# A four-layer attention block on one core: layer sums regrouped, value staging moved, far masks shared with GpSimd, loads throttled

## The chip, the cores and the metric

The kernel runs on one core of one Trainium2 chip. The metric is the device time of one execution in microseconds (us), lower is better. Each figure is the median of several executions, and each kernel was run beside the kernel before on the same chip. Ratios are the mean time of one kernel's fast runs over the mean of the other's fast runs of the same rounds, so not quite the ratio of the medians quoted beside them. The span of a profiled execution is 1 to 3 us shorter than its time.

TensorE (PE in the profile) has two rows: matmuls (PE) and the loading of the stationary operand (PEld). VectorE is DVE, ScalarE is ACT, GpSimd is POOL, and SP issues transfers.

## The reference

Sequence 2048, width 512, 32 heads of 16. Layers 1 and 3 are linear attention (A), layers 2 and 4 are causal softmax attention over a window of 256 keys (B).

```python
def A(x, wqkv, wo):                      # q, k, v: 32 heads of 16
    phi = lambda t: where(t > 0, t + 1, exp(t)) + 1e-6
    pq, pk = phi(q), phi(k)
    kv = einsum("hsd,hse->hde", pk, v)   # a sum over all 2048 tokens
    z  = pk.sum(over tokens)
    o  = einsum("hqd,hde->hqe", pq, kv) / (einsum("hqd,hd->hq", pq, z) + 1e-6)
    return o @ wo
def B(x, wqkv, wo):
    s = q @ k.T / 4;  keep 0 <= query - key < 256
    return softmax(s) @ v @ wo
x = A_x
x = x + A(layernorm(x));  x = x + B(layernorm(x))
x = x + A(layernorm(x));  x = x + B(layernorm(x))
```

Because `kv` sums over all tokens, nothing of layer 3's output can start before layer 2 is complete: there is a barrier in the middle.

## The kernel before

The kernel is a list of operations, each with what it reads and writes. A compressed table (`TABLE`) fixes for all of them their order on each engine, the engine where there is a choice, and the PSUM bank. Tokens go in 16 tiles of 128. Per tile and layer B there are edge scores (two blocks of 64 keys, up to 256 queries each) and, for 14 tiles, far scores (64 queries per key block, at the far end of the window, with a triangular mask).

Layer A multiplies the query features by a reciprocal that one matmul group (`spread`) copies from 8 heads to 128 rows, tile by tile:

```python
def a_out(self, t, key):
    for f in range(4):        # 4 full-array matmuls of 128 columns
        e.matmul(K.ps(ps)[:, f*P:(f+1)*P], K.spread[:, tg, f, :], K.rec[:, G, :], ...)
    ... tensor_tensor(K.pqd, K.ps(ps), K.XQ[tile], ALU.mult)   # VectorE
```

The loads are issued one after another without waiting; the order is x0, x1, x2-3, wAk, x4-5, wAv, x6-7, wAq, the rest of x, then the other weights. In layer 1 each token tile has a key, a value and a query projection, and the keys times values are summed after that.

The softmax here doesn't subtract the row's maximum and nothing guards it: scores larger than these inputs give would overflow.

## Time and profile before

| | before |
|---|---|
| median of 4 runs of the comparison | 432.88 us (432.72 to 434.98) |
| span of the profiled run, mean granted clock | 432.7 us, 0.987 |
| ScalarE idle in the two attention stretches | 5.9 and 2.5 us |

I cut traces at four events: the first exponential of layer 2, the last one of it, the first of layer 4, the last of it. So the five windows are: start with the first layer, attention of layer 2, barrier, attention of layer 4, tail. The columns are the stretch and its length, then busy time and count of PE, PEld, DVE, ACT and POOL, then granted clock, DMA share and GB/s. Kernel before:

```profile
0.00:73.50 73.50, 63.43 (x683) 41.24 (x684) 62.46 (x140) 32.76 (x60) 39.91 (x83) 1.00 0.44 117
73.50:239.40 165.90, 160.76 (x3219) 102.48 (x3218) 154.16 (x353) 160.00 (x231) 22.22 (x52) 1.00 0.42 85
239.40:276.80 37.40, 37.13 (x600) 29.40 (x599) 30.21 (x67) 16.57 (x32) 9.56 (x18) 1.00 0.06 20
276.80:425.20 148.40, 137.21 (x3024) 90.35 (x3023) 124.48 (x273) 145.93 (x204) 11.64 (x25) 0.97 0.41 95
425.20:432.70 7.50, 3.54 (x62) 1.97 (x59) 3.41 (x8) 0.01 (x1) 0.00 (x0) 0.92 0.12 38
```

ScalarE is full in the second and fourth window (160.00 of 165.90, 145.93 of 148.40), TensorE in the third (37.13 of 37.40). A saving counts only in the window whose full engine it relieves.

### The profile page before, as it was taken

How to read it: one execution, taken by the hardware profiler on the slowest of the kernel's cores; microseconds unless marked ns; L12 is line 12 of the kernel's file. 1: busy time of each engine (PE TensorE's matmuls, PEld its weight loads, DVE VectorE, ACT ScalarE, POOL GpSimd, SP SyncE). 2: the span in 40 equal slices, each digit the busy share in tenths (PEclk: the TensorE clock that was granted, in tenths of full speed). 3: DMA queues.
4: the chain of work that ended last, by engine and by line, in shares of the span. 5: the costliest groups of instructions: out<-in, count | busy, mean ns of one | idle time of the engine just before them, and what ended most of it. 6: DMA issues, size and time to landing. Idle time of an engine off the chain costs nothing.

```text
span 432.7 us, 17332 instructions
## 1 busy us (share of the span) xinstructions
PE 402.1 (93%) x7576; PEld 265.4 (61%) x7576; DVE 374.7 (87%) x838; ACT 355.3 (82%) x525; POOL 83.3 (19%) x177
## 2 busy tenths in 40 slices
PE   1999999999999999999999999999999999999675
PEld 0555777655665665655656778765667576666443
DVE  5997799999999999988988679999899898987545
ACT  1454546999999999999998443799999999999982
POOL 7789112011120111111000141111000101000000
PEclk9999999999999999999999999999999999999869
DMA  7635104424443555545421000234344443436321
GB/s 241 220 64 148 49 2 106 97 65 97 117 84 82 78 102 101 89 78 107 97 53 26 15 3 2 88 102 102 91 105 94 105 102 101 90 100 101 92 53 51
DMA packets 69292, 37.84 MB, mean 87 GB/s; under 512 B 49248, under 2 KB 64608, under 8 KB 69216
## 3 DMA queue, kind: packets, MB, share of 16 engines
q1 hardware_dynamic: 69216, 36.73, 36.9%
q8 instruction: 60, 0.98, 1.0%
q14 instruction: 16, 0.13, 0.1%
HBM read 6.29 MB, written 2.10 MB: 19 GB/s over the span
## 4 chain that ended last, share of the span: by engine, by line
PE 43%; ACT 41%; DVE 9%; DMA 3%; issue 1%; POOL 1%; SPq 1%; POOLq 0%
ACT pb L549 31%; PE ps L351 19%; PE ps L365 10%; ACT pb L583 7%; PE ps L608 6%; PE ps L535 3%; DMA xres<-in_A_x_dram 2%; ACT pb L550 2%; PE ps L402 1%; DVE stats L312 1%; ACT tE L374 1%; DVE xres L478 1%; DMA xT<-xn 1%; DVE xn L316 1%; PE ps L573 1%
## 5 line engine op out<-in xcount | busy, mean ns | idle before, releaser
L549 ACT ACTIVATE pb<-ps 128x1024 bf16<-128x1024 f32 x224 | 211.1, 1050 | 3.7 <-PE ps L535 2.7
L608 PEld LDWEIGHTS ps<-vB,pb 128*128 128x128 bf16 x2880 | 80.3, 96 | 16.8 <-issue 3.9
L608 PE MATMUL ps<-vB,pb 128*128 128x34 bf16 x2880 | 86.8, 178 | 2.0 <-ACT pb L549 1.0
L314 POOL TENSOR_SCALAR ve<-mv 128x1 f32<-128x1 f32 x64 | 18.1, 283 | 285.3 <-DVE mv L313 284.1
L351 PE MATMUL ps<-wA,XQ 128*128 128x512 bf16 x256 | 65.9, 387 | 3.2 <-DMA wA<-in_A_wqkv_dram 2.8
L365 PE MATMUL ps<-xT,wBp 128*128 128x128 bf16 x1024 | 66.9, 219 | 1.6 <-DVE o L620 0.5
L374 ACT ACTIVATE tE<-ps 128x512 bf16<-128x512 f32 x64 | 38.1, 605 | 35.6 <-PE ps L351 16.9
L365 PEld LDWEIGHTS ps<-xT,wBp 128*128 128x128 bf16 x1024 | 58.2, 98 | 9.5 <-issue 1.7
L583 ACT ACTIVATE pb<-ps 128x512 bf16<-128x512 f32 x112 | 60.8, 642 | 1.6 <-PE ps L573 1.2
L556 DVE TENSOR_TENSOR pb<-pb,tri 128x512 bf16<-128x512 bf16 x128 | 52.2, 415 | 8.6 <-ACT pb L550 4.3
L535 PE MATMUL ps<-XQ,kB 32*128 32x256 bf16 (+3 forms) x1024 | 49.9, 270 | 8.4 <-ACT pb L550 2.6
L478 DVE TENSOR_TENSOR xres<-ps,xres 128x512 bf16<-128x512 f32 x64 | 43.7, 684 | 5.9 <-PE ps L351 5.4
L312 DVE BATCH_NORM_STATS2 stats<-xres 128x6 f32<-128x512 bf16 x64 | 43.6, 686 | 5.5 <-DMA xres<-in_A_x_dram 4.8
L590 DVE TENSOR_TENSOR pb<-pb,tri 128x1024 bf16<-128x1024 bf16 x56 | 37.5, 678 | 1.3 <-ACT pb L583 1.3
L315 POOL TENSOR_TENSOR rs<-ve,negh 128x1 f32<-128x1 f32 x64 | 37.6, 587 | 5.3
L535 PEld LDWEIGHTS ps<-XQ,kB 32*128 32x128 bf16 x1024 | 15.3, 92 | 37.7 <-ACT pb L549 17.9
L351 PEld LDWEIGHTS ps<-wA,XQ 128*128 128x128 bf16 x256 | 21.7, 98 | 26.4 <-issue 4.9
L351 PE MATMUL ps<-wBo,oT 128*128 128x512 bf16 x128 | 35.2, 388 | 1.3 <-DVE oT L335 0.5
L365 PE MATMUL ps<-XQ,wA 128*128 128x128 bf16 x512 | 35.5, 219 | 0.0
L351 PE MATMUL ps<-M,pqd 128*128 128x512 bf16 x128 | 34.6, 380 | 0.5 <-DVE pqd L472 0.5
L365 PEld LDWEIGHTS ps<-XQ,wA 128*128 128x128 bf16 x512 | 30.9, 98 | 6.6 <-issue 0.4
L351 PE MATMUL ps<-wBv,xT 128*128 128x512 bf16 x128 | 33.9, 381 | 0.7 <-DVE vA L495 0.4
(77 smaller groups left out, 453.7 us busy)
## 6 DMA issues: line engine op xcount, KB each, us to landing
vB<-vA SPq DMA_DIRECT2D x128, 68.0 KB, 2.1
kB<-vA SPq DMA_DIRECT2D x64, 128.0 KB, 2.1
out_dram<-xres SPq DMA_DIRECT2D x16, 128.0 KB, 2.5
wA<-in_A_wqkv_dram SPq DMA_DIRECT2D x3, 512.0 KB, 9.4
xres<-in_A_x_dram SPq DMA_DIRECT2D x2, 512.0 KB, 8.1
pb<-in_B_wqkv_dram SPq DMA_DIRECT2D x1, 1024.0 KB, 9.6
xres<-in_A_x_dram SPq DMA_DIRECT2D x3, 256.0 KB, 3.8
wBv<-in_B_wqkv_dram SPq DMA_DIRECT2D x1, 512.0 KB, 4.3
```

What stands on the lines that cost most here:

```text
L312: self.on("DVE", "stats", lambda e: e.bn_stats(K.stats[:, t, :], K.xres[:, t, :]), key, dve(512), rd=[("xres", t)], wr=[("stats", t)])
L315: self.on("POOL", "pow", lambda e: e.tensor_tensor(K.rs[:, t, :], K.ve[:, t, :], K.negh[:], ALU.pow), key + 0.03, (640, 690), rd=[("ve", t ...
L351: m = e.matmul(K.ps(ps), lhs(c), rhs(c), start=c == 0, stop=c == 3)
L365: m = e.matmul(K.ps(ps)[:, f * P:(f + 1) * P], w(c, f), xT(c), start=c == 0, stop=c == 3)
L374: self.on("ACT", "E", lambda e: e.activation(K.tE[:, s, :], K.ps(ps), ACT.Exp, bias=0.0), key, act(512), wr=[("tE", s)], ps=[ps])
L478: self.on("DVE", "res", lambda e: e.tensor_tensor(K.xres[:, t, :], K.ps(po), K.xres[:, t, :], ALU.add), key, dve(512), rd=[("xres", t)], w ...
L535: m = e.matmul(K.ps(ps[gq])[:, 256 * b:256 * b + ns[b]], K.kB[rows, j % 4, 2 * f + b, :, :], K.XQ[rows, f, q:q + ns[b]], start=True, stop= ...
L549: return e.activation(x, bank().rearrange("p g (b n) -> p g b n", b=2), ACT.Exp, bias=0.0, scale=0.25)
L556: return e.tensor_tensor(x, x, K.tri[:, 0, :].unsqueeze(1).unsqueeze(1).to_broadcast([P, 4, 2, 64]), ALU.mult)
L583: return e.activation(K.pb[:, sl, 2 * h:2 * h + 2, :, o:o + 64], i, ACT.Exp, bias=0.0, scale=0.25)
L590: return e.tensor_tensor(x, x, K.tri[:, 1, :].unsqueeze(1).to_broadcast([P, 16, 64]), ALU.mult)
L608: m = e.matmul(K.ps(ps)[:, 34 * u:34 * u + 34], K.pb[:, (b // 2) % 3, gq, f, o:o + P], K.vB[:, (b // 2) % 4, b % 2, r, :], start=i == 0, s ...
```

## The change

The intent: fewer and wider ScalarE and VectorE operations in attention, some masks moved to GpSimd, TensorE work taken out of layer 1 and out of the barrier, and a start that gets the key weights sooner. The core of the diff, cut (left out: the two keys of a pair lie interleaved in `kB`, and the masks and value transfers follow):

```diff
@@ loads: at most three in flight, key weights third in the list (the table issues them second)
-  seq += [x0, x1, x2-3, wAk, x4-5, wAv, x6-7, wAq, x8-11, x12-15, wAo, wBn] ...
+  seq += [x0, x1, wAk, x2-3, wAq, x4-5, x6-7, x8-11, x12-15, wAv, wAo, wBn, wBv, wBo]
+  begun.append(self.load(n, f, b, r, key + i if i < 6 else 100.5 + 0.5 * i,
+                         begun[max(0, i - 3):i - 2] if i >= 3 else []))
@@ TensorE: nine matmuls on zeros before the first real one
+  for _ in range(9): e.matmul(self.PS[:, 7, :], warm[:, 0:P], warm, ...)
@@ layer 1: sum normalised x (xn) times key features, then value weights
-  self.a_v(t, k + 0.05)                                # per tile
+  e.matmul(K.ps(acc[c]), xn(t)[:, c*P:(c+1)*P], K.pk[:, t, :], start=t == 0, stop=t == T-1)
+  ... four copies, then 16 matmuls with wA[:, c, 1024:]
@@ spread: one group of 16 matmuls in four row tiles for four token tiles
-  e.matmul(K.ps(ps)[:, f*P:(f+1)*P], K.spread[:, tg, f, :], K.rec[:, G, :], ...)   # a_out, per tile
+  for f in range(4):
+    for tg in range(4):
+      e.matmul(K.ps(bc[tg])[:, f*P:(f+1)*P], K.spread[rows, f, :], K.rec[rows, G, :],
+               ..., tile_position=(32 * tg, 0))
+  ... XQ multiplied in place, four times
@@ value staging of layer B in a buffer of its own (vS), so vA is free
-  room = self.roomv[st]          # six tiles of vA
+  room = [("vS", st)]
+  if j >= LATE: self.a_v(j, ...)  # LATE = 5: layer 3's values of tiles 5..15 in attention
@@ far part: two exponentials of 1024; masks on either engine
-  for b in range(2): ... exp of 512, wr=[("F", sl, h, b)]
+  ... exp of 1024, wr=[("F", sl, h)]
+  if eng == "POOL": return e.affine_select(out=x, in_=x, compare_op=ALU.is_ge, ...)
+  self.g.add("mf", engs, mk, ..., rd=[("F", sl, 0), ("F", sl, 1), ("tri",)], ...)
@@ edge scores of the last tiles up to four head groups wide; last output in halves (b_last)
   TABLE replaced
```

## The prediction

> **What bounds the kernel now.** I read the page's busy times first, then a table of windows that I cut where the slices change character, then the chain of waits inside one window, then the timeline of the start.
>
> ```profile
> PE 402.1 (93%) x7576; PEld 265.4 (61%) x7576; DVE 374.7 (87%) x838; ACT 355.3 (82%) x525; POOL 83.3 (19%) x177
> ```
>
> Three engines stand above 80%, so no single average names the bound. The windows do (columns: stretch, then busy time and instruction count of PE, PEld, DVE, ACT, POOL, then clock and DMA):
>
> ```profile
> 12.00:62.00 50.00, 49.09 (x515) 30.73 (x513) 44.91 (x97) 25.17 (x47) 28.34 (x52) 1.00 0.37 96
> 62.00:90.00 28.00, 27.11 (x430) 19.29 (x427) 26.88 (x62) 21.24 (x30) 4.69 (x12) 1.00 0.36 82
> 90.00:225.00 135.00, 130.29 (x2680) 83.06 (x2677) 125.42 (x289) 131.84 (x180) 19.68 (x46) 1.00 0.45 90
> 225.00:240.00 15.00, 15.00 (x282) 9.05 (x281) 13.38 (x33) 11.90 (x33) 1.14 (x3) 1.00 0.17 35
> 240.00:277.00 37.00, 36.73 (x594) 29.13 (x591) 29.81 (x64) 16.71 (x32) 9.23 (x18) 1.00 0.06 20
> 277.00:284.00 7.00, 7.00 (x88) 4.23 (x85) 6.61 (x16) 6.80 (x9) 0.79 (x2) 1.00 0.38 98
> 284.00:411.00 127.00, 119.37 (x2684) 78.85 (x2676) 110.42 (x241) 126.30 (x163) 10.83 (x22) 0.99 0.42 99
> 411.00:433.00 22.00, 14.18 (x316) 9.14 (x316) 10.66 (x25) 12.63 (x35) 0.00 (x0) 0.81 0.22 51
> ```
>
> There are four kinds of stretch. ScalarE is full in the two attention stretches (131.84 of 135 and 126.30 of 127). It is half idle in the first linear layer (25.17 of 50) and in the barrier before the third layer (16.71 of 37). Inside the second attention stretch the chain consists of exponentials (start, length, what):
>
> ```profile
> 290.26 7.44 ACT pb L549 x8
> 297.70 1.96 ACT pb L583 x4
> 299.66 0.01 issue
> 299.67 7.44 ACT pb L549 x8
> 307.11 1.96 ACT pb L583 x4
> ```
>
> Eight exponentials of 1024 columns take 7.44 us, 0.93 each; the four far ones of 512 take 1.96, 0.49 each. One token tile is 9.40 us, and next to nothing else is on the path.
>
> PE shows busy nearly everywhere, so I recount its need from back-to-back runs: a 512-column matmul 0.223 us (28 in 6.24), a 128-column one 0.056 (16 in 0.89), a 34-column one 0.028 (48 in about 1.37), a one-column one 0.025. From 12 to 62 us that gives some 134 x 0.216 + 273 x 0.056 + 64 x 0.025 + 2 = 48 of 50 us. From 90 to 210 us it gives about 105 of 120. From 228 to 272 us it gives 44 of 44. So **PE bounds the first layer and the barrier, ScalarE bounds the attention**, and PE has about an eighth to spare there. VectorE is a close second in attention (125 of 135).
>
> The start is a fourth regime. In the timeline (start, length, engine, line, op):
>
> ```profile
> 9.31 1.86 PE L351 MATMUL ps<-wA,XQ 128*128 128x512 bf16 x4 [2.81 <-DMA wA<-in_A_wqkv_dram]
> ...
> 9.91 0.69 DVE L312 BATCH_NORM_STATS2 stats<-xres 128x6 f32<-128x512 bf16 x1 [1.75 <-DMA xres<-in_A_x_dram]
> ...
> 12.15 1.07 DVE L316 TENSOR_SCALAR xn<-xres,mv,rs 128x512 bf16<-128x512 bf16 x1
> 12.22 0.85 POOL L284 TENSOR_SCALAR_AFFINE_SELECT spread<-spread 128x512 bf16<-128x512 bf16 x1
> ...
> 15.06 6.24 PE L351 MATMUL ps<-wA,XQ 128*128 128x512 bf16 x28 [0.39 <-DVE pk L376]
> ```
>
> PE waits for the key weights until 9.31 us although they were issued at 2.70; then four matmuls take 1.86 us, and from 15.06 on four take 0.89.
>
> **What the Trainium skill says.** (1) "Perfetto Trace Analysis", Identifying the Most-Contended Engine: matmul busy time is a poor measure of how near PE is to its limit. The trace agrees: 130 busy of 135 in attention, where the recount needs 88%. (2) "ScalarE: Activation LUTs", What ACT_TABLE_LOAD costs: 0.833 ns per column, 186 ns fixed, neighbours overlapping by about 93. The trace gives a smaller fixed part: (2 x 0.49 - 0.93) = 0.055 us per instruction in a run, and I use that. (3) "SBUF — State Buffer", Who interferes with whom: a VectorE op in a two-port mode, or with two SBUF inputs against a GpSimd op that reads SBUF, blocks or is blocked for the whole instruction. The trace agrees: the normalising op took 1.07 us beside a 0.85 us affine select, against a median of 0.406. (4) "TensorE: Matmul & The Clock Gate", Part 3, Measured speedup vs the span model: four row tiles of K=32 ran 3.07 times as fast as one after another. Here eight 32-row score matmuls of 256 columns stand 0.33 us apart from the next work, which shows the same concurrency.
>
> **The change, part by part.**
> Loads: at most three in flight, and the key weights third, before the bulk of x. Ahead of them lie 256 KB; the 768 KB at the 241 GB/s of the first slice take 3.2 us after an issue near 2, so the weights should land at about 6 instead of 9.3. Nine dummy matmuls warm PE, so the first twelve 512-column ones need not run at 0.46 us. Both together: **-4** (3 for landing, 1 for the slow matmuls, of which VectorE, full from 10 to 30 us, may take some back).
> First layer: it drops 64 value matmuls (64 x 0.22 = 14.1) and 64 of 128 columns (3.6); it adds 64 of 512 columns (14.1) and 16 of 128 (0.9). PE saves 2.7 us. Sixteen evictions become four (12 x 0.6 = 7.2 us off ScalarE and VectorE). But the sum must now be evicted (two rounds of 0.6), multiplied by the weights (0.9) and only then masked: about 2.3 us of new serial latency. Query projections can fill part of it on PE. Net **-1.5**.
> Spread matmuls: 64 per phase of 128 columns, full array (64 x 0.056 = 3.6 us), become four concurrent row tiles, at 3 to 4 times the speed: 2.5 us less per phase. In attention that is slack; in the two turnovers it counts for **-1** in all.
> Value staging in its own buffer: the GpSimd clearing of 4 x (1.03 or 1.07 us) at each turnover halves, and eleven of sixteen value projections of the third layer move from the barrier into attention. That takes 11 x 0.88 = 9.7 us off a stretch where PE needs all of its time, and fills about half of PE's spare eighth of 150 us (19 us). The barrier's own latency chain (residual at 247.2, first exponential at 276.75) does not shrink with it, so I count **-7**.
> Far exponentials: two of 1024 for four of 512 saves 4 x 0.49 - 2 x 0.93 = 0.1 us per tile, x 28 tiles = 2.8. The edge groups (64 small ones) become 24 wider ones: by the same fit 10.5 to 9.4 us per phase, 2.2 in all. Together **-5**, nearly all on the path, though the end of the last phase has gaps.
> Far masks: 56 x 0.68 = 37.5 us of VectorE may go to GpSimd. Its affine select took 0.852 us for 512 columns and 0.240 for 64, so about 1.55 for 1024 (estimate from these two). VectorE is off the path, so this mainly lets it take copies now done by ScalarE in the attention of the second layer (some 6 us there outside the exponentials): **-2**.
> Last tile in halves: the tail from 427.3 is transpose 0.4, copy 0.4, matmul 1.0, add 0.7, store. Half-sized pieces shorten it by about **-1**.
> Sum: -4 - 1.5 - 1 - 7 - 5 - 2 - 1 = -21.5, so 432.9 - 21.5 = 411.4; I say **412**.
>
> **Rivals.** (a) PE becomes the bound in the second layer's attention: the moved projections lift its need from 88% to about 93% of a shorter stretch, in strict order with the scores. For it: PE's few waits now. Against it: the scores need only about 2 us per tile. It would return 4 to 7 us: about 418. (b) The shared port: 56 selects of 1.55 us are 87 us in which the normalising op and the near masks (128 x 0.415, two SBUF inputs) may stand. VectorE would lose what it gained and ScalarE would wait for masks only through values, late. For it: the 1.07 us pair above. Against it: GpSimd is used 15% in attention and the schedule may leave masks on VectorE. About 416 to 420. (c) The four accumulators hold four of eight PSUM banks through the first layer, leaving four for keys and queries; each key bank is held through matmul, exponential and feature op, about 3 us. Sixteen keys and some queries in four banks need 25 to 30 us of 45, so I expect no bound, but if the query work is pushed behind the sums, +4: 416. (d) All shortened parts were on the path, queries fill the new latency, and the barrier gives back the full 9.7: about 405.
>
> **Range and chances.** Errors of the parts are about 2 us each for the start and first layer, 4 for the barrier, 3 for the attention, so some 6 together; rivals add more on the slow side. Range 402 to 422. Two per cent is 8.7 us, at 424.2; only (a), (b) and (c) together would keep it above that. Faster 0.92, same 0.07, slower 0.01.
>
> **What would show it.** The first real key matmul near 6 us with 0.22 us spacing; the first attention exponential 6 to 7 us earlier than 73.46; the barrier's gap in attention exponentials (from 239 to 276.75 us now) down by 5 to 9; attention tiles of about 9.3 us in the last phase; far exponentials as 1024 columns at 0.93; a tail of about 4.5 us after the last value matmul. I am wrong if VectorE ops lengthen beside GpSimd selects and ScalarE shows waits in attention, if the gap of the barrier stays near 37 us, or if the first layer ends no sooner because VectorE carries it.

## More of the kernel before

The far part of B, for one tile; `h` counts pairs of the four head groups, `b` the two key blocks:

```python
def b_far(self, j, key):
    ...                       # 32 matmuls of 64 columns into four banks, c = 256*b + 64*f
    for h in range(2):
        for b in range(2):    # four exponentials of 512 columns
            self.on("ACT", "ex", exp(pb[h, :, b] <- ps), wr=[("F", sl, h, b)], ...)
    for b in range(2):        # two masks, each over all heads of one key block
        self.on("DVE", "mk", tensor_tensor(x, x, K.tri[:, 1, :]..., ALU.mult),
                rd=[("F", sl, 0, b), ("F", sl, 1, b), ("tri",)], ...)
```

## The result

The changed kernel is **slower**: 437.96 us (437.38 to 438.25, four runs) against 432.88, a ratio of 1.0104 with a 95% interval of 1.0072 to 1.0137. By the 2% rule that is "same". The predicted 412 and the whole range of 402 to 422 are missed.

The busy line of the changed kernel, to be held against the first line of the prediction:

```profile
PE 401.0 (92%) x7539; PEld 258.8 (59%) x7539; DVE 358.8 (82%) x803; ACT 346.1 (79%) x427; POOL 105.4 (24%) x194
```

ScalarE lost 9.2 us of work, VectorE 15.9 and TensorE 1.1. The five windows of the changed kernel:

```profile
0.00:72.90 72.90, 63.90 (x637) 37.97 (x637) 58.90 (x135) 28.18 (x49) 37.78 (x82) 0.95 0.51 118
72.90:238.50 165.60, 158.67 (x3217) 101.80 (x3218) 148.14 (x339) 156.70 (x186) 33.99 (x61) 1.00 0.37 85
238.50:279.80 41.30, 39.81 (x653) 29.12 (x651) 36.54 (x78) 19.01 (x35) 6.85 (x14) 1.00 0.08 18
279.80:426.10 146.30, 133.05 (x2926) 86.04 (x2926) 111.65 (x245) 141.42 (x156) 26.80 (x37) 0.95 0.39 95
426.10:435.70 9.60, 5.58 (x110) 3.82 (x110) 3.60 (x8) 0.79 (x3) 0.00 (x0) 0.76 0.14 44
```

| window | before | after | difference |
|---|---|---|---|
| start and layer 1 | 73.5 | 72.9 | -0.6 |
| attention, layer 2 | 165.9 | 165.6 | -0.3 |
| barrier | 37.4 | 41.3 | +3.9 |
| attention, layer 4 | 148.4 | 146.3 | -2.1 |
| tail | 7.5 | 9.6 | +2.1 |
| span | 432.7 | 435.7 | +3.0 |

The table holds 3.0 of the 5.1 us between the medians: the profiled execution of before took 434.41 us, 1.5 above its median, that of after 437.38, the fastest of its four.

In the two attention windows ScalarE's work fell by 3.3 and 4.5 us (160.00 to 156.70 and 145.93 to 141.42), but the windows shrank by only 0.3 and 2.1. The rest became idle time: 5.9 to 8.9 us and 2.5 to 4.8 us. The chain of waits of the changed kernel in the second attention shows both, with columns start, length and what:

```profile
294.16 1.46 PE ps L654 x48
295.62 0.46 PE ps L367 x8
296.08 0.36 PE ps L580 x8
...
296.46 3.77 ACT pb L590 x4
300.23 1.83 ACT pb L622 x2
302.06 7.34 ACT pb L590 x8
```

From 300.23 on a tile costs 1.83 + 7.34 = 9.17 us instead of 9.40: the wider far exponentials do their work. But up to 296.44 the chain lies on TensorE: value products (L654), a projection (L367) and then the scores (L580) that the exponential waits for. Over this whole window the chain lies on TensorE for 56.6 us (38.1 before) and on ScalarE for 73.3 (108.8). The waits of ScalarE's exponentials for a TensorE result in the stretch of 72 to 426 us, first before, then after (engine, what waits, for what: microseconds in all, times, longest):

```profile
ACT pb L550 <- PE ps L535: 3.1, 6, 1.1
ACT pb L549 <- PE ps L535: 2.7, 8, 0.6
ACT pb L583 <- PE ps L573: 1.2, 2, 0.6
```

```profile
ACT pb L590 <- PE ps L580: 6.7, 13, 1.6
ACT pb L590 <- PE ps L654: 2.4, 1, 2.4
ACT pb L622 <- PE ps L613: 1.2, 3, 0.5
```

Seven microseconds become 10.3. So the gain in attention was mostly turned into waits, the barrier grew, the tail grew, and the start gained next to nothing. The experiments take these one by one.

### The profile page after: what moved, and what is told of

Same layout as the page of the kernel before. It is cut to its first block, busy times and chain, and to the rows that moved or that the text cites. A ratio compares the mean times of both kernels' runs of the same rounds, so it can differ in the third digit from the quotient of the medians.

```text
span 435.7 us, 17184 instructions
## 1 busy us (share of the span) xinstructions
PE 401.0 (92%) x7539; PEld 258.8 (59%) x7539; DVE 358.8 (82%) x803; ACT 346.1 (79%) x427; POOL 105.4 (24%) x194
## 4 chain that ended last, share of the span: by engine, by line
PE 45%; ACT 38%; DVE 9%; DMA 6%; issue 1%; SPq 0%; DVEq 0%; ACTq 0%
ACT pb L590 29%; PE ps L353 15%; PE ps L367 10%; PE ps L654 9%; ACT pb L622 7%; PE ps L580 4%; PE ps L426 3%; DMA xres<-in_A_x_dram 2%; DVE stats L314 2%; ACT tE L376 1%; DMA XQ<-vA 1%; DVE xres L519 1%; DVE XQ L508 1%; PE ps L613 1%; DMA xT<-xn 1%; DMA kB<-vA 1%
## 5 line engine op out<-in xcount | busy, mean ns | idle before, releaser
L590 ACT ACTIVATE pb<-ps 128x1024 bf16<-128x1024 f32 (+1 forms) x248 | 233.9, 1053 | 9.7 <-PE ps L580 6.7
L654 PEld LDWEIGHTS ps<-vB,pb 128*128 128x128 bf16 x2880 | 80.2, 97 | 19.3 <-DVE pb L596 7.6
L654 PE MATMUL ps<-vB,pb 128*128 128x34 bf16 x2880 | 86.4, 179 | 2.5 <-DVE pb L596 1.2
L316 POOL TENSOR_SCALAR ve<-mv 128x1 f32<-128x1 f32 x64 | 15.7, 245 | 225.8 <-DVE mv L315 224.3
L367 PE MATMUL ps<-xT,wBp 128*128 128x128 bf16 x1024 | 67.8, 219 | 1.1 <-DMA xT<-xn 0.7
L596 DVE TENSOR_TENSOR pb<-pb,tri 128x512 bf16<-128x512 bf16 (+1 forms) x124 | 52.8, 430 | 16.0 <-ACT pb L590 15.2
L367 PEld LDWEIGHTS ps<-xT,wBp 128*128 128x128 bf16 x1024 | 58.4, 98 | 11.4 <-issue 2.7
L580 PE MATMUL ps<-XQ,kB 32*128 32x256 bf16 (+3 forms) x1024 | 49.7, 272 | 10.7 <-ACT pb L590 6.8
L622 ACT ACTIVATE pb<-ps 128x1024 bf16<-128x1024 f32 x56 | 55.4, 1064 | 1.2 <-PE ps L613 1.2
L353 PE MATMUL ps<-wA,XQ 128*128 128x512 bf16 x192 | 52.0, 390 | 4.0 <-DMA XQ<-vA 2.1
L630 POOL TENSOR_SCALAR_AFFINE_SELECT pb<-pb 128x1024 bf16<-128x1024 bf16 x22 | 29.6, 1346 | 61.1 <-ACT pb L622 60.9
L580 PEld LDWEIGHTS ps<-XQ,kB 32*128 32x128 bf16 x1024 | 15.3, 93 | 41.7 <-ACT pb L590 23.2
L317 POOL TENSOR_TENSOR rs<-ve,negh 128x1 f32<-128x1 f32 x64 | 36.5, 570 | 5.3
L367 PE MATMUL ps<-XQ,wA 128*128 128x128 bf16 x512 | 35.7, 220 | 0.0
L367 PEld LDWEIGHTS ps<-XQ,wA 128*128 128x128 bf16 x512 | 31.0, 98 | 6.2 <-issue 0.5
L353 PE MATMUL ps<-M,XQ 128*128 128x512 bf16 x128 | 33.2, 381 | 0.2
L353 PEld LDWEIGHTS ps<-wA,XQ 128*128 128x128 bf16 x192 | 16.4, 99 | 22.1 <-DMA XQ<-vA 2.6
```

The lines of the kernel that those rows point to most:

```text
L317: self.on("POOL", "pow", lambda e: e.tensor_tensor(K.rs[:, t, :], K.ve[:, t, :], K.negh[:], ALU.pow), key + 0.03, (640, 690), rd=[("ve", t ...
L353: m = e.matmul(K.ps(ps), lhs(c), rhs(c), start=c == 0, stop=c == 3)
L367: m = e.matmul(K.ps(ps)[:, f * P:(f + 1) * P], w(c, f), xT(c), start=c == 0, stop=c == 3)
L580: m = e.matmul(K.ps(ps[gq])[:, ns * i:ns * i + ns], K.kB[rows, j % 4, 2 * f + b, :, :], K.XQ[rows, f, q:q + ns], start=True, stop=True, ti ...
L590: return e.activation(out(2 * h, 2, ns), i, ACT.Exp, bias=0.0, scale=0.25)
L596: return e.tensor_tensor(x, x, K.tri[:, 0, :].unsqueeze(1).unsqueeze(1).to_broadcast([P, 4, n, 64]), ALU.mult)
```

## The experiments

In an edit "on after" or "on before" the order table is kept as far as the operations allow; where only the table changes, that is said. All runs were correct. "Windows" are the five lengths in the order of the table above.

### The start

`loads_around`, on after: no throttle, the loads issued as fast as SP can, the late weights sent after the seventh and eleventh transposes of x.

```diff
-  begun.append(self.load(n, f, b, r, key + i if i < 6 else ..., begun[max(0, i-3):i-2] if i >= 3 else []))
+  self.load(n, f, b, r, key + i, [])
```

> The changed kernel with only its fourteen loads moved: no load waits for another; the token tiles, the query and key weights of layer 1 and the weight for the folding first, the layer-1 value and output weights behind the seventh transpose, the layer-2 ones behind the eleventh. Theory (the throttled loads keep the queues busy to 29 us, so the first transposes land late and TensorE loses about 5 us of work between 15 and 62 us): the transpose line that took 5.68 us goes back to about 2.5, first attention exponential 3 to 6 us earlier than 72.9, whole kernel 433 to 435 us. Rival (layer 1 is held by VectorE and the PSUM copies, the loads are hidden): start within 1 us, kernel 437 to 439.

Measured: 436.39 us (434.84 to 437.61), ratio to before 1.0055 (1.0014 to 1.0096); windows 69.9, 165.4, 41.3, 146.8, 9.6. The first window is 3.0 us shorter than in after, the others are within 0.5. By the medians the kernel gains 1.6 us, and the two intervals overlap. The chain of the throttled kernel shows where the start lost time:

```profile
19.27 5.68 DMA XQ<-vA
...
24.99 1.89 PE ps L353 x4
```

A transpose of a normalised tile (XQ<-vA) goes by DMA and takes 5.68 us, while the throttled loads still land (the last at 31.57 us). The granted clock is then 0.50 for 3.41 us, so the four products behind it take 1.89 instead of about 0.86. The unthrottled kernel has one such piece of 5.53 us as well, later (from 31.68, beside its late weights), but its two pieces of 128 KB of x land in 2.1 us in the median instead of 3.3 and its first key product starts at 7.11 instead of 8.51. The size of the throttle's cost is measured; the way through these waits is read, not tested. Over all runs with this first layer and no new order from 62 us on, the first attention exponential comes at 72.9, 72.6, 74.7 and 75.0 with the throttle, at 69.9, 70.0, 71.9 and 71.0 without: means of 73.8 and 70.7. The three such profiles with before's first layer have 72.8 in the mean. So the rest of the new start is worth some 2.1 us and the throttle costs 3.1. One order varies by about 2.5 us here, so these are sizes to within a microsecond or so.

`loads_warm25`, on loads_around: 25 warming matmuls for 9.

```diff
-                    for _ in range(9):
+                    for _ in range(25):
```

> loads_around with 25 warm-up matmuls in place of 9, so that TensorE has no pause between the last of them and the first key product at 8.5 us. Theory (nine end at 5 us, TensorE idles 2.5 us and the first real products run at half speed all the same): first products in 0.43 us in place of 0.85 to 1.03 a pair, first attention exponential 0.5 to 1.5 us earlier than 69.9, time 434.5 to 436. Rival (the products wait for data in the start anyway): start within 0.3 us, 436 to 437.

Measured: 437.54 us (434.57 to 440.23), 1.0075 (1.0021 to 1.0129); first attention exponential at 70.0 against 69.9. In the timeline (start, length, engine, line, operation, count) of loads_warm25:

```profile
1.24 6.97 PE L882 MATMUL ps<-kB 128*128 128x512 bf16 x25 [1.24 <-DVE kB L877]
...
9.12 0.61 PE L352 MATMUL ps<-wA,XQ 128*128 128x512 bf16 x2 [0.69 <-ACT XQ L336]
```

The same place in loads_around, with nine:

```profile
1.25 4.02 PE L882 MATMUL ps<-kB 128*128 128x512 bf16 x9 [1.25 <-DVE kB L877]
...
7.11 0.60 PE L352 MATMUL ps<-wA,XQ 128*128 128x512 bf16 x2 [0.69 <-ACT XQ L336]
...
10.30 1.91 PE L352 MATMUL ps<-wA,XQ 128*128 128x512 bf16 x4
```

The first pair of products is as fast with nine (0.60 us) as with 25 (0.61). But with nine TensorE stands idle three times around it (0.75, 0.69 and 0.87 us), and from 9.02 to 12.43 the granted clock is 0.50: four products take 1.91 us. With 25 it stays at 1.00. In after the clock was granted at 4.51 us, during the last of the nine, and taken back at 7.93, behind 2.47 us of idle time, so that its first pair, at 8.51, takes 1.03. The Trainium skill, "TensorE: Matmul & The Clock Gate", Part 1, says that a window of about 3.4 us of activity releases the clock and an idle one takes it back. The trace agrees in the length: the low stretches here last 3.41 us. So nine matmuls do get the clock granted, and the pauses behind them lose it again; in spread_by_tile, with the same nine, it came only at 13.03. Fast products brought nothing: the first sums stand at 15.00 with 25, at 15.28 with nine. In these two profiles the start waits for loads and VectorE, not for TensorE's clock. The later 4 us that this run lost are told in the last section.

### The value projections and the barrier

`values_early`, on after, table only: the value halves of layer 3's tiles 5 to 11 directly behind their keys in the attention, with the copies on VectorE.

> The changed kernel with the layer-3 value projections of tiles 5 to 11 moved up to directly behind the keys of the same tile, their copies onto VectorE; four halves thereby leave the barrier, where 12 of 32 were. Theory (the barrier is held by TensorE's work, 38.9 us of 41.3, so each half taken out is 0.43 us): barrier 41.3 goes to about 39 to 39.8, the late attention a little shorter too, time 435 to 437. Rival (TensorE is as full in the attention as in the barrier, so the work only moves): barrier shorter, layer-2 attention longer by as much, 437.5 to 439.

Measured: 445.37 us (443.43 to 447.22), 1.027 (1.0217 to 1.0323); windows 75.0, 171.1, 41.1, 147.6. Attention lost 5.5 us, ScalarE's idle time in it rose from 8.9 to 14.5, and the barrier gained 0.2. The work was moved, not removed, into a stretch that had no room; and the barrier, with four halves (1.7 us) less to do, hardly shrank.

That led to a count of what each order really did. Half a value projection is two matmuls of 512 columns, 0.44 us. Before the change 22 of the 32 halves already ran inside the attention of layer 2 (between 211 and 236 us) and 10 in the barrier. After the change it is 20 and 12: the new buffer allows more, the new table does less. Three query halves of layer 1 moved from the start into the attention (27 ran before its first exponential before, 24 after), and 24 query halves of layer 3 ran after its last exponential before, 17 after. TensorE's need, counted as operations times their back-to-back spacing, is 149.7 us in the attention and 36.3 in the barrier before, 147.9 and 38.9 after; in sum 186.0 and 186.8. There was no TensorE work to be won. The 2.6 us more in the barrier are the two value halves (0.9) and, above all, last value products, output and key projections that now come behind the last exponential (about 3.4 net), less the query halves that left it (1.7).

`barrier_first`, on loads_around, table only between 231 and 281 us: the last tile's value products and its transpose ahead of most projections. One theory was that the barrier is the latency chain behind the last exponential, the other that it is TensorE's work.

> loads_around with the order changed between 231 and 281 us alone, so that the last tile's four value products and its transpose come ahead of most query and value projections. Theory A (the chain from the last values to the first scores of layer 4 sets the barrier; last tile's values end 4.7 us later after the last exponential than before the change): barrier 41.3 goes to 38 to 39. Theory B (TensorE's work of 38.9 us sets it, with 2.6 us idle): 39.5 to 40.5. The replay says about 39.3. Time 434 to 435.5.

Measured: 436.58 us (435.48 to 437.49), 1.0063 (1.0023 to 1.0103); windows 71.0, 165.7, 41.8, 147.0. The division of the last tile's values now ends 5.9 us after the last exponential instead of 7.7 (3.0 in before). But what follows came later: the last key-value product starts 21.9 us after that exponential (21.4 in after, 16.1 before), and the barrier is no shorter. The edit shortened the head of the chain and not the chain, so this run decides nothing.

The kept traces decide more. In microseconds, from the last exponential of layer 2:

| run | last key-value product starts | barrier ends | between |
|---|---|---|---|
| before | 16.1 | 37.4 | 21.3 |
| after | 21.4 | 41.3 | 19.9 |
| values_early | 21.2 | 41.1 | 19.9 |
| pair_slack (below) | 20.0 | 39.4 | 19.4 |
| before_pair_slack2 (below) | 15.9 | 36.1 | 20.2 |

In every run except spread_by_tile and three_mends, which split the spread, the last column lies between 19.3 and 21.4. values_early is the test: 1.7 us of TensorE's work less, the product 0.2 us earlier, the barrier 0.2 shorter. So the barrier follows the chain to that product and not the amount of work. Of the 5.3 us that the product is late in after, 4.7 are there when the last tile's values are divided. The wider edge scores may be why: with four head groups in one exponential, all four value products of the last tile stand behind the last exponential, where two did before. That is read from the programs and traces; no run narrowed them in layer 2.

The part behind that product changed too. In before it is nearly all TensorE; in after, at its start:

```profile
260.69 0.60 DVE pqd L468
261.29 0.96 DVE recf L492
...
264.32 1.79 DVE XQ L508 x3
266.11 0.66 DVE xres L519
```

The grouped form needs four tiles' reciprocals before one multiplication can start, so VectorE steps stand in a row where matmuls stood. But this part became 1.4 us shorter in all, so it does not explain the growth.

### The far exponentials, alone

`before_far_1024`, on before: only the far part changes, to two exponentials of 1024.

```diff
-                        c = 256 * b + 64 * f
+                        c = 128 * f + 64 * b
-            for b in range(2):
-                def ex(e, h=h, b=b): ...   # 512 columns
+            def ex(e, h=h): ...            # both key blocks, 1024 columns
```

> The kernel before with one term of the change alone: the far scores of a tile go through two exponentials of 1024 columns in place of four of 512, everything else and the order kept. Theory (the attention of layer 4 is held by ScalarE, 145.9 us busy of 148.4; 28 tiles each lose two instructions of about 0.05 us fixed cost): ScalarE's work falls by about 0.1 us a tile, so about 2.8 us over both layers, time 430 to 432. Rival (TensorE or the banks hold the attention, and a bank pair comes back later when its exponential is longer): within 0.7 us of before, 432 to 433.5.

Measured: 437.99 us (437.16 to 438.73), 1.0107 (1.0074 to 1.0139). ScalarE's busy time fell from 355.3 to 352.5, exactly the 2.8 us that the prediction had counted, and the kernel became 5 us **slower**; windows 72.9, 168.1, 37.4, 150.0. The groups of far masks on VectorE show why (count, busy time, mean ns; then the engine's idle time ahead of them and what ended it). Before, then before_far_1024:

```profile
L590 DVE TENSOR_TENSOR pb<-pb,tri 128x1024 bf16<-128x1024 bf16 x56 | 37.5, 678 | 1.3 <-ACT pb L583 1.3
```

```profile
L593 DVE TENSOR_TENSOR pb<-pb,tri 128x1024 bf16<-128x1024 bf16 x56 | 37.7, 681 | 6.0 <-ACT pb L586 6.0
```

A mask covers one key block of all heads. With four exponentials the table runs both of block 0 first, so its mask is free after two short ones; with two long ones it needs both. That makes it one long exponential later. VectorE, which keeps its order, stands still for it, and so do the copies and additions behind it. In before the four run from 131.86 to 134.02 and the first mask starts at 133.07; in before_far_1024 the two run from 132.19 to 134.22 and the mask starts at 134.25:

```profile
133.07 0.69 DVE L590 TENSOR_TENSOR pb<-pb,tri 128x1024 bf16<-128x1024 bf16 x1
133.68 0.68 DVE L472 TENSOR_TENSOR pqd<-ps,XQ 128x512 bf16<-128x512 f32 x1
```

```profile
134.25 0.69 DVE L593 TENSOR_TENSOR pb<-pb,tri 128x1024 bf16<-128x1024 bf16 x1 [0.81 <-ACT pb L586]
134.86 0.68 DVE L476 TENSOR_TENSOR pqd<-ps,XQ 128x512 bf16<-128x512 f32 x1
```

The product behind it (pqd), which the next layer-A output needs, is late by 1.2 us.

`before_far_pair`: the same, and each mask over both key blocks of one pair, so that it reads one exponential only.

```diff
-        for b in range(2):                  # mask of 16 x 64, reads both exponentials
+        for h in range(2):                  # mask of 8 x 2 x 64, reads exponential h
-  rd=[("F", sl, 0, b), ("F", sl, 1, b), ("tri",)]
+  rd=[("F", sl, h, 0), ("F", sl, h, 1), ("tri",)]
```

> The kernel before with the two exponentials of 1024 columns as in the run before_far_1024, and with the two far masks cut by head pair in place of by key block, so that each mask needs one exponential and not both; count and size of masks as before. Theory (the merged exponentials lost because a mask by block waits for both of them and VectorE's queue stands behind it: its idle time before far masks went from 1.3 to 6.0 us): that idle time goes back to about 2 us, time 430 to 433. Rival (fewer, longer exponentials themselves hold the banks longer): 436 to 438.5 as in before_far_1024.

Measured: 433.55 us (433.14 to 436.8), 1.0001 (0.996 to 1.0043); windows 72.1, 166.0, 37.4, 149.0. The wait is gone:

```profile
L592 DVE TENSOR_TENSOR pb<-pb,tri 128x1024 bf16<-128x1024 bf16 x56 | 37.5, 677 | 0.6 <-ACT pb L586 0.6
```

This pair of runs is the clearest: same arithmetic, same instruction count, same banks and same order on all engines but for which of a tile's two masks VectorE runs first, and 4.4 us apart by what a mask reads. But the loss is only undone; the 2.8 us are not won yet.

`loads_pair`, on loads_around: the same pairing in the changed kernel, where 22 of the 56 far masks run on GpSimd. One theory expected the gain to carry over, its rival none, since VectorE waits little for these masks there.

```diff
-        for b in range(2):
+        for h in range(2):
-  rd=[("F", sl, 0), ("F", sl, 1), ("tri",)]
+  rd=[("F", sl, h), ("tri",)]            # on GpSimd as two selects of half the size
```

> loads_around with its far masks cut by head pair in place of by key block; those on GpSimd become two instructions of half the size. Theory (a mask by block waits for both merged exponentials, as in the kernel before): attention of layer 2 and 4, 165.4 and 146.8, each 1 to 2.5 us shorter, time 432.5 to 435. Rival (in the changed kernel 22 masks stand on GpSimd, out of VectorE's queue, so little waits): within 1 us of loads_around, 435.5 to 437.

Measured: 434.88 us (433.81 to 437.07), 1.0032 (0.9985 to 1.0078); windows 71.9, 165.2, 41.3, 147.2, in attention as loads_around (165.4, 146.8). By the windows the rival was right: attention, where the theory put the gain, did not shrink. The median, 1.5 us below loads_around, falls in the theory's range, but the two intervals overlap. The group lines of after fit the rival: VectorE lost 2.7 us there, not 6.0.

```profile
L630 POOL TENSOR_SCALAR_AFFINE_SELECT pb<-pb 128x1024 bf16<-128x1024 bf16 x22 | 29.6, 1346 | 61.1 <-ACT pb L622 60.9
L631 DVE TENSOR_TENSOR pb<-pb,tri 128x1024 bf16<-128x1024 bf16 x34 | 24.0, 717 | 2.7 <-ACT pb L622 2.4
```

### The masks on GpSimd

`masks_vector`, on after, table only: all 56 far masks on VectorE.

> The changed kernel with all far masks on VectorE (22 of 56 ran on GpSimd). Theory (VectorE has 18 per cent to spare over the run, the masks on GpSimd give little): VectorE 22 times about 0.6 us busier, time within 1.5 us of the changed kernel, 437 to 439. Rival A (the masks on GpSimd are what keeps VectorE off the path, worth the 2 us that was predicted): 439.5 to 442. Rival B (GpSimd's masks hold VectorE up by sharing its access to SBUF): 434 to 436.5.

Measured: 440.79 us (437.56 to 442.36), 1.0162 (1.0107 to 1.0217), which the 2% rule leaves unclear; windows 74.7, 166.0, 41.3, 149.0. The run loses steadily against after, from 1.2 us at the first attention tile, where nothing differs, to 5.0 at the last: some 3.7 us for the 22 masks, 2.8 by the medians. But that profile is the slowest of its four and after's the fastest, and the two intervals just overlap, so the size is rough; it does not speak against the prediction's -2. The masks take 1.35 us each on GpSimd (1.55 estimated). Those left on VectorE last 717 ns in the mean beside them and 682 without, so sharing costs little here.

### The spread matmuls

`spread_by_tile`, on after: the group of 16 matmuls split into four of four, each just before its multiplication.

```diff
-  one operation: for f in range(4): for tg in range(4): e.matmul(..., tile_position=(32*tg, 0)), ps=bc
+  for tg in range(4):
+    own operation: for f in range(4): e.matmul(..., tile_position=(32*tg, 0)), ps=[bc[tg]]
```

> The changed kernel with each spread of four banks cut into four of one bank, each issued just before the multiply that uses it. Theory (one spread takes four banks that come back only as four multiplies of 0.6 us end, so the scores wait and ScalarE idles 1.0 to 1.6 us at each of five spreads in the attention): idle ScalarE in the two attention stages 8.9 and 4.9 us falls to about 6 and 3, kernel 433.5 to 435. Rival (the banks were not the limit; TensorE is, and 24 more small groups cost it about 1 us): 437 to 439.

Measured: 449.15 us (445.55 to 450.09), 1.0336 (1.0283 to 1.0389): 11 us worse than after; windows 76.8, 167.2, 46.2, 148.3; TensorE's busy time rises by 12.6 to 413.6. Its timeline, against the grouped one of after:

```profile
157.09 0.39 PE L501 MATMUL ps<-rec,spread 32*128 32x128 bf16 x4
157.41 0.62 PE L367 MATMUL ps<-xT,wBp 128*128 128x128 bf16 x8
```

```profile
109.34 0.40 PE L501 MATMUL ps<-rec,spread 32*128 32x128 bf16 x16 [0.29 <-ACT pb L590]
109.67 1.37 PE L654 MATMUL ps<-vB,pb 128*128 128x34 bf16 x48
```

Sixteen in four row tiles stand 0.33 us before the next operation; four in one row tile stand 0.32, since they run one after another and the array is switched twice. Half a projection (two full-array matmuls of 512 columns or eight of 128) stands 0.43 to 0.45 us before other full-array work and 0.52 to 0.54 before a row-tiled group: about 0.1 us for a switch. The Trainium skill, "TensorEngine Tiling (Array Packing)", Key Properties, says that changing the tiling mode drains TensorE and gives no figure; the trace agrees. So grouping is right: it saves 4 x 0.22 - 0.33 - 0.1, some 0.45 us a group of four token tiles.

`spread_mixed`, on after: three of the eight groups taken tile by tile with a full-array constant, built by GpSimd in idle buffers. The theory was that a group holds four PSUM banks and so delays the scores.

> The changed kernel with the three spreads that fall inside the attention (two of layer 2, one of layer 4) taken one tile at a time over the full array as before the change, one bank each; the five of the start and the barrier stay grouped. Theory (the grouped spread holds four banks and costs ScalarE 1.6, 1.2 and 0.9 us of waiting; the per-tile one in row tiles failed only because each switch to row tiles and four serial matmuls cost TensorE 0.43 us): ScalarE's idle time falls by 2 to 3.5 us, TensorE gains about 1.3 us of work, time 434.5 to 436.5. Rival (ScalarE's waits were only where another shortage showed): 437.5 to 439.

Measured: 448.55 us (446.48 to 449.18), 1.0343 (1.0304 to 1.0381); windows 79.0, 166.1, 41.3, 151.4. It lost 10.6 us, of which building the constants took a part (the start alone is 6 us longer). Attention of layer 2 is 0.5 us longer, not shorter, so the run gives the bank theory no support and can't refute it. ScalarE does wait 0.9 to 1.6 us beside some of these groups in after; why stays open.

### The last tile

`last_narrow`, on after: edge exponentials of the last tile in two head groups instead of four.

```diff
-  wide = [min(4, 512 // min(256, S - P*j - 64*b)) for b in range(2)]
+  wide = [min(2 if last and j == T-1 else 4, 512 // min(256, S - P*j - 64*b)) for b in range(2)]
```

> The changed kernel with the last token tile's edge scores in groups of two head groups in place of four, in layer 4 alone: two more score groups, four more exponentials, two more masks, so that the first half waits only for the first half of tile 14's values and the last value products are half as many. Theory (the wide groups make the last exponentials wait 2.36 us for tile 14's second half): last exponential to end 9.6 goes to about 8, kernel 435 to 436.5. Rival (the end is set by the chain of divide, transpose, copy, product and store alone; the extra exponentials cost what the wait did): 437.5 to 439.

Measured: 439.33 us (437.5 to 439.93), 1.0118 (1.0081 to 1.0155); tail 9.0. A wait of 2.65 us ahead of the last exponentials stays, so the width wasn't its cause. The tails differ in another thing, the granted clock. Before, then last_narrow:

```profile
425.00:430.00 5.00, 3.74 (x70) 2.17 (x66) 3.41 (x8) 0.21 (x2) 0.00 (x0) 1.00 0.11 33
```

```profile
425.00:430.00 5.00, 4.10 (x112) 3.33 (x109) 1.99 (x5) 1.66 (x4) 0.00 (x0) 0.50 0.22 55
```

After has 0.76 in its whole tail and four value products after the last exponential, before one. Which of the two costs the 2.1 us I did not separate.

### All mends together

`three_mends`, on after: loads_around, spread_by_tile and last_narrow at once.

> The three edits together. Theory (three separate losses on the path): gains add, 3 to 6 for the loads, 3 for the spreads, 2 for the end, so 427 to 431 us and faster than the kernel before. Rival (TensorE's work bounds the attention and an earlier start is given back as waits for it): less than half of the sum, 434 to 437.

Measured: 444.85 us (444.06 to 445.5), 1.0251 (1.0211 to 1.029); windows 73.2, 167.1, 44.6, 149.1. It is 4.3 us faster than the split spread alone: the split spread loses far more than the loads win.

### The order itself

None of this explains why the changed kernel doesn't use its smaller need. So I replayed both orders with the durations that the traces show and let a search move single operations, keeping the arithmetic. `after_reordered` (on loads_around) and `before_reordered` (on before) are the first results. Both change the table only, from 62 us on.

> loads_around with the same operations, but in another order, on other banks and engines from 62 us on: found by replaying the order with the durations of the traces and moving single operations as long as the replayed end came earlier. The replay gives 432.2 us for the span of loads_around (433.1 measured) and 423.9 for this one: layer-2 attention 161.4 in place of 166.0, barrier 41.4, layer-4 attention 143.1 in place of 145.6. Theory (the change's work is small enough, its order throws the gain away): time 425 to 430, faster than before. Rival (a replay misses what two engines do to each other; any other order loses, as four of the edits did): 434 or more.

> The kernel before, its order from 62 us on moved in the same way and with the same effort: replayed span 423.9 against 430.6 for its own order (432.7 measured). Theory (order is worth as much for the kernel before, so the change itself brings about what its earlier first exponential brings, 3 to 4 us, and no more): 424 to 429. Rival (the order of before was already the best that the chip gives): 432 or more.

Measured: 453.82 us (452.82 to 456.38), 1.0472 (1.0432 to 1.0511), and 447.61 us (444.35 to 451.2; the 451.2 was slow, without it 447.47), 1.0284 (1.0238 to 1.033). The replay had promised 423.9 for each; in after_reordered ScalarE stood idle for 18.8 and 13.7 us in its two attentions. TensorE's waits for operands that come by DMA tell what it had wrong; the columns are microseconds, times and longest, first after_reordered, then loads_around:

```profile
PE ps L366 <- DMA xT<-xn: 8.0, 9, 1.9
```

```profile
PE ps L366 <- DMA xT<-xn: 0.4, 1, 0.4
```

The search had placed each user of a transposed tile just where a typical transfer lands; a real one is often later, and TensorE, strictly in order, stands. TensorE's matmuls wait 13.7 us for transposes by DMA in after_reordered, 4.3 in loads_around and 0.8 in before. (The 23 and 7 of the forecast below add the waits of both its rows, and so count some twice.) Before's order has slack where it matters.

So the next replay reckoned with late hand-overs: 4.2 us for a transpose by DMA, 3.4 for a copy by DMA, and longer signals. `pair_slack` is loads_pair with such an order, `before_pair_slack` is before_far_pair with one.

> loads_pair, its order from 62 us on moved by replay as in after_reordered, but with 4.2 us reckoned for a transpose to land, 3.4 for a copy and slower hand-overs. Theory (after_reordered lost because transposes were used as they landed, 23 us of TensorE's waiting on them against 7): those waits under 5 us, time 426 to 433. Rival (the replay misses something else, between engines or in TensorE's prefetch): 437 or more.

> before_far_pair, re-ordered with the same slack and effort. Theory: 425 to 431, as much gain as for the changed kernel, so that order, not the change, decides. Rival: 436 or more.

Measured: 435.98 us (435.62 to 436.56), 1.0054 (1.0012 to 1.0097), and **430.56 us** (429.77 to 431.63), 0.9927 (0.9888 to 0.9966). The second is the first kernel below before. Its attentions are 166.8 and 147.1, its barrier 35.6. In pair_slack TensorE's waits for transposes fell to 2.7 us, as forecast, and the barrier to 39.4, but attention rose to 167.9 and the time stayed: late transposes were not all that the replay had wrong.

Is that the order alone? `before_slack` re-orders before, without the change of the far part, in the same way; `before_pair_slack2` starts the re-ordering at 25 us instead of 62.

> The kernel before with its own operations, re-ordered from 62 us on with the same slack and effort as before_pair_slack; the replay with slack gives 432.3 from 441.0, against 426.5 from 438.1 for before_pair_slack. Theory (the merged exponentials with masks by head pair are worth about 3 us once the order fits them): 432 to 435, no better than before. Rival (the order alone brings the gain): 428 to 431.5.

> before_pair_slack re-ordered further, from 25 us on; the replay with slack falls from 427.8 to 423.9. Theory (slack keeps the replay true): 426 to 429.5, the fastest of all. Rival (the last microseconds of the replay are again found where the chip does not follow): 430 to 434.

Measured: before_slack 433.94 us (433.03 to 435.0), 0.9994 (0.9966 to 1.0021), so this new order without the far change is worth nothing. before_pair_slack2 **429.19 us** (428.54 to 429.79, six runs) against 433.79 (eleven runs), 0.9891 (0.9873 to 0.9909). It beats both kernels. Its second to fourth windows (the tail takes 8.8 us):

```profile
71.60:236.50 164.90, 156.52 (x3201) 104.31 (x3233) 150.47 (x351) 159.78 (x207) 23.30 (x53) 1.00 0.38 85
236.50:272.60 36.10, 34.99 (x554) 27.60 (x559) 31.12 (x67) 16.20 (x31) 9.40 (x18) 1.00 0.06 17
272.60:418.60 146.00, 132.88 (x3012) 91.00 (x3039) 123.70 (x273) 143.78 (x178) 10.28 (x24) 0.94 0.40 92
```

ScalarE is idle for 5.1 and 2.2 us in its attentions, as little as before, with 2.4 us less work. (The trace lacks about 80 matmul records, so the PE columns are a little low.) So the wider far exponentials are worth their 2.8 us, when the masks read one each **and** the order fits: alone they cost 5, with the masks mended 0, with both they win 3. That rests on one found order of each kind. The 4.6 of before_pair_slack2 also hold what ordering from 25 us on is worth by itself, which no run separates.

A last sum over the boundary, attention of layer 2 plus barrier, says what mends were only shifts: before 203.3, after 206.9, loads_around 206.7, values_early 212.2, barrier_first 207.5, pair_slack 207.3; before_pair_slack 202.4, before_pair_slack2 201.0. No order that I tried for the changed kernel got under 206, so its loss of 3.6 us there is a cost of its order, of its wide last edge groups or of its grouped spread, and which of them stays open.

## Why the prediction was wrong

The sum was -21.5; +5.1 was measured in the medians, +3.0 in the spans. By the prediction's own steps:

- **Bounds.** TensorE is busy for 37.1 of 37.4 us in the barrier, but its work does not set the length: in the changed kernel values_early took 1.7 us of it out for 0.2 us. In attention ScalarE's work fell and most of it came back as waits, so it was not the only bound there either.
- **Barrier, -7: this is the step that failed.** It rests on the sentence that eleven of sixteen value projections "move from the barrier into attention", a stretch "where PE needs all of its time". I read the first half off the diff and did not look where the old order had them. The trace of before had 22 of 32 halves in attention already; the change moved two of them the other way. The second half failed as well: four halves less in values_early made the barrier 0.2 us shorter and the attention 5.5 longer. The window measures +3.9, and it follows the chain to the last key-value product, which starts 21.4 us after the last exponential instead of 16.1. My own falsifier, "the gap of the barrier stays near 37", came true and worse.
- **Loads, -4.** 3 us of it were for an earlier landing. The key weights did land at 5.80 us, about the 6 that I counted. The first key product still came at 8.51 instead of 6, and the throttle undid the gain: with the weights early but the loads throttled the window is 0.6 us shorter in the profiled pair, and 1.0 longer by the means of all profiles. Taking the throttle out gives 3.1 us. I counted when the weights land and not what else waits for the same queues, the transposes by DMA (5.68 us on the chain). The 1 us for a warm clock was 0 by loads_warm25; nine matmuls got the clock granted and did not keep it.
- **First layer, -1.5, and spread, -1.** Without the throttle the start with the first layer is about 2.1 us shorter, where loads and layer together were given -5.5. The grouped spread saves 4 x 0.45 = 1.8 us of TensorE a layer instead of the 2.5 counted, since the switch of modes was left out.
- **Far exponentials and edge groups -5, masks -2.** The sizes were right. ScalarE's busy time fell by 7.8 us in the two attentions against 7 predicted; before_far_1024 alone measured 2.8 for 2.8, and masks_vector, roughly, 3 us for 2. (Of the fixed cost, 2 x 0.49 - 0.93 is 0.05 us and not 0.055.) What failed is "nearly all on the path": 5.3 us of the 7.8 came back as ScalarE idle time, 2.4 arrived. In before_far_1024 the mechanism is shown, a mask that now waits for both exponentials. In the changed kernel it is not that one (loads_pair left both attention windows as they were) but scores that come late, and I could not name one cause for it.
- **Last tile, -1.** The tail grew by 2.1 us: three more value products stand after the last exponential, and the granted clock is 0.76 instead of 0.92. How much each costs is open.
- **Rivals.** (a) is nearest: the scores come late in attention, though TensorE's need didn't rise. (b) is not borne out: without GpSimd's masks, in masks_vector, the kernel is no faster. (c) was not tested; three query halves did move behind the first exponential, as it feared. (d) did not happen. None of the four had the throttle or a longer barrier in it, and all of them started from a sum that was too good.
- **Range.** The errors of the parts were treated as independent and small. They shared one assumption, that a new order keeps all the slack of the old one.

## What to carry to other kernels

Before counting work as moved out of a stretch, look in the trace where the old order has it; a diff says what is allowed and the trace what is done. When instructions are merged, go through their readers: a reader that needed half now waits for the whole, and pairing the readers with the merged pieces may decide what the merge is worth: here it cost 5 us or nothing, and won 3 in an order made for it. An engine that is busy all through a stretch need not set its length; take a little work out and see whether the stretch shrinks. In a kernel with a fixed order, a change of operations and a fitting order belong together, and an order found by replay needs slack for hand-overs that arrive late.

## What the Trainium skill lacked or had wrong

- No page tells what merging activations does to their readers: a mask over half of each of two merged exponentials made VectorE idle 6.0 us instead of 1.3 ahead of 56 masks, and the kernel 5 us slower; masks paired with the exponentials made it 0.6.
- "TensorEngine Tiling (Array Packing)", Key Properties, names the drain at a change of tiling mode without a size. Here it is about 0.1 us a switch, and splitting eight groups of 16 row-tiled matmuls into 32 of four cost 11 us.
- "ScalarE: Activation LUTs", What ACT_TABLE_LOAD costs, has 186 ns fixed with 93 overlapping, which leaves 93. In runs of exponentials here it was 50 ns per instruction (2 x 0.49 - 0.93 us), and the saving computed from that (2.8 us) was measured as 2.8.
- "TensorE: Matmul & The Clock Gate", Part 1, lets an idle window take the clock back. Here windows that were idle only in part did so: in the 3.4 us before the drop at 7.93 in after TensorE was busy for 0.83 us, in those before a drop at 198.66 in loads_warm25 for 2.05. There TensorE stood idle for 2.62 us from 197.30, the granted clock was 0.50 for 6.83 us, and this execution, the slowest of four, was 4 us late from there. (A transpose that landed in 2.5 us in loads_around took 4.6 just before; whether it began the pause is not shown.) First loads_warm25, then loads_around in the same stretch:

```profile
200.00:205.00 5.00, 5.00 (x25) 1.22 (x25) 2.33 (x5) 3.12 (x4) 0.00 (x0) 0.50 0.00 0
```

```profile
200.00:205.00 5.00, 4.81 (x117) 3.42 (x118) 3.92 (x9) 4.32 (x6) 0.00 (x0) 1.00 0.30 84
```

- No page says how late a transpose by DMA may land beside loads: 5.68 us at the start of after, and TensorE's matmuls lost 13.7 us to waits for transposes in an order that reckoned with typical durations.
